# A graph tensor product on one core: other distances between engines in a hand-ordered stage, and one holder for a shared accumulator bank

## The chip, the core and the metric

One core of one Trainium2 chip runs the kernel as one program. Its engines are TensorE (PE: matmuls, whose weight loads have a row PEld of their own), VectorE (DVE), ScalarE (ACT), GpSimd (POOL: here it issues indirect DMAs) and SyncE (SP: it issues plain DMAs). Each engine works off its own list of instructions in order and waits at semaphores for the others. The metric is the device time of one execution in microseconds; lower is better.

## The reference

There are 10000 nodes with 64 channels of 4 components each, and 640000 edges in no order. Every edge takes the row of its source node, forms a small tensor product with its own 4 numbers Y, scales it per channel, and is added to its destination node; at the end the channels are mixed.

```python
N, deg, C, L, DE = 10000, 64, 64, 1, 4          # E = N * deg, M = 4
R = _silu(edge_feat @ w_rad)                              # (E, C)
xs = x[src]                                               # (E, C, M)
tp = jnp.einsum('eci,ef,ifo->eco', xs, Y, cg)             # (E, C, M)
msg = R[:, :, None] * tp
agg = _segment_sum(msg.reshape(-1, C * M), dst, N).reshape(N, C, M)
return jnp.einsum('ncm,cd->ndm', agg, w_mix)
```

## The kernel before

**Sorting.** Edges are brought together by destination in two passes of a radix sort through DRAM. A pass counts, for chunks of 12 tiles of 128 edges, how many edges go to each of 18 digits (`count`, matmuls on one-hots into the bank `cnt`), turns the counts into destinations (`tables`, L290 to L377), and then moves the edges (`route`, L379 to L493). The first pass (`pass1`) sorts by group of 576 nodes and writes to `grp`; the second (`pass2`) sorts a group by bucket of 32 nodes and writes to `bkt`. The edges are handled in two parts, 49% and 51%, so that the first pass over the second part can run beside messages of the first.

**A route** has one chunk per step. `prepare` makes the one-hot D of a quad (two chunks); `places` puts the position of every edge into the accumulator bank `pp` by matmuls, and in the same step ScalarE copies it out as `pc`; `slots` turns it on VectorE into a row and a slot; `spread` builds on VectorE the shifted payload X and most of the one-hots oh, and on ScalarE the last five tiles of oh (squares `sq`, then a ReLU); `move` multiplies them on PE into the bank `pr`; `evict` copies it to `rt` on ScalarE; `store` issues the scatter on POOL, LS = 8 steps after `spread`. In step k the order is evict(k-3), move(k-2), places, spread(k), slots, store(k-8), so X and oh of chunk k take the buffers that move(k-2) gives back where they have two (X), and those of move(k-3) where they have three (oh). `pp` has one buffer and `pr` two, and both are shared by the two routes that run side by side.

**Messages** (`messages`, L644 to L782) go by units: half a bucket, 4 tiles of edges in the first part of the edges and 5 in the second, 626 units in each. Per unit: `gather` issues one indirect DMA per tile on POOL into one of 6 buffers xg; `turn` transposes the payload on PE into a bank `pre` (two buffers), `turned` copies it out on ScalarE as sT, `radial` multiplies it on PE with the radial weights into the same bank, where ScalarE applies SiLU in place; `spots` builds S on VectorE from the destination and Y; `products` multiplies the gathered rows by the radial values in place on VectorE; `sums` adds the unit up on PE in the bank G (one buffer, two units per bucket); `evict` copies G to Gs on ScalarE; every fourth bucket `mix` multiplies by the mixing weights on PE into the bank `po`, and ScalarE or VectorE brings the result to `ot`, which SP writes to the output. A unit is issued in four quarters, in an order written out by hand (L775):

```python
quarters = (((index, LI), (gather, LG), (products, 0), (turn, 1)), ((sums, -1), (turned, 1)),
            ((radial, 1), (spots, 1)), ((evict, -1), (mix, -2)))
```

The number is the unit's offset from the running one.

**What sets the order.** In the main phase (from L931) PE, VectorE and ScalarE take exactly the order in which the program issues; POOL and SP are put in order by a planner. `groups` (L787) issues one quarter of `messages` after another, and ahead of each quarter as many steps of the other two generators as their rates allow: `later` is the first pass over the second part of the edges (about 0.14 steps per quarter, up to the quarter `total`), `sort` is the second pass for the segment that comes next (48 steps over about 144 quarters). In the phase before it only SP keeps the written order. `weave` runs a step of the next block's counting (`front`) beside each step of a first-pass route. All the small matmuls (cnt, offp, ovp, dp, po) share one accumulator bank, "misc"; who comes next waits at its semaphore.

Of the kernel before, what the change touches and what calls it, by code (L numbers as in the profile page):

```python
# [17 lines left out]
F = mybir.dt.float32  # L18
# [6 lines left out]
P = 128  # L25
# [10 lines left out]
LG = 4  # L36
LI = 8
# [15 lines left out]
def weave(main, side, ratio):  # L53

    acc = 0.0
    for _ in main:
# [5 lines left out]
    for _ in side:  # L62
        yield
# [7 lines left out]
class Kernel:  # L71
    def __init__(self, ctx, tc, x, src, dst, Y, ef, w_rad, cg, w_mix, out):
# [49 lines left out]
        self.tab = {}  # L122

# [166 lines left out]
    def tables(self, ps, N, cs, carry, kov, carry2, kov2, base, cap):  # L290
# [14 lines left out]
        yield  # L305
# [47 lines left out]
        yield  # L353
# [14 lines left out]
        yield  # L368
        dp = self.ps.tile([P, 512], F, name="dp", tag="misc", bufs=1)
        nc.tensor.transpose(dp[:, :N], val[:N, :], self.ident[:N, :N])  # L370
        idx = wk.tile([P, P], I32, name="idx", tag="idx" + ps.key, bufs=2)
        ds = dest
        nc.scalar.activation(ds[:, :N], dp[:, :N], AF.Copy)
        yield
# [4 lines left out]
    def route(self, ps, quad, nt, sb, idx):  # L379

        nc, wk, tc, T, Q = self.nc, self.ph, self.tc, ps.T, ps.Q
        N = (nt + T - 1) // T
        QD, PP, MS, XO, PR, RT = {}, {}, {}, {}, {}, {}
# [4 lines left out]
        def places(q):  # L388
# [17 lines left out]
            for u in range(full * T, m - 1):  # L406
# [3 lines left out]
                             Dq.rearrange("p t b -> p (t b)"), start=False, stop=True)  # L410
            pc = PP[q] = wk.tile([P, Q * T, B], F, name="pc", tag="pc" + ps.key, bufs=1)
# [15 lines left out]
        def spread(c):  # L427
# [6 lines left out]
            X = self.ph.tile([P, T, ps.rw], F, name="X", tag="X" + ps.key, bufs=2)  # L434
# [4 lines left out]
            oh = self.ph.tile([P, T, P], F, name="oh", tag="oh" + ps.key, bufs=3)  # L439
# [31 lines left out]
        prepare(0)  # L471
        yield
        places(0)
        yield
        slots(0)
        yield
# [18 lines left out]
    def pass1(self, part, first, size):  # L495
# [16 lines left out]
        def front(o, m):  # L512
# [8 lines left out]
            for a in range(0, m, QT):  # L521
# [3 lines left out]
                yield  # L525
                cnt = self.ps.tile([P, 512], F, name="cnt", tag="misc", bufs=1)
                self.count(cnt, ps, D, a // T, z - a, N, True, True)
                w = min(T, z - a) * B
# [63 lines left out]
    def pass2(self):  # L592
# [11 lines left out]
        for i, (k, g) in enumerate(self.segs):  # L604
# [19 lines left out]
            N = (nt + ps.T - 1) // ps.T  # L624
            cnt = self.ps.tile([P, 512], F, name="cnt", tag="misc", bufs=1)
            for a in range(0, nt, 8 * ps.T):
                z = min(a + 8 * ps.T, nt)
                self.count(cnt, ps, D[:, a:z], a // ps.T, z - a, N, a == 0, z == nt)
            cs = ph.tile([P, ps.T * B], F, name="cs2", bufs=1)
            nc.scalar.activation(cs[:N], cnt[:N, :ps.T * B], AF.Copy)  # L630
            yield
# [8 lines left out]
    def pass2_steps(self, k, g):  # L640
        return (self.gt[k][g] + 27) // 28 + (self.gt[k][g] + 11) // 12 + LS + 20


    def messages(self):  # L644
# [60 lines left out]
        def radial(k):  # L705
# [3 lines left out]
            nc.scalar.activation(R, R, AF.Silu)  # L709
# [45 lines left out]

        def mix(k):
# [211 lines left out]
```

## Time and profile before

| | us |
|---|---|
| median of 3 runs | 10343.14 (10334.53 to 10346.17) |
| the profiled execution | 10335.18, its span 10333.0 |
| PE busy | 8440.1 (82% of the span) |
| VectorE busy | 7318.8 (71%) |
| ScalarE busy | 3553.8 (34%) |
| POOL busy | 6272.0 (61%) |
| gathers: 5634 indirect DMAs | 5345.3, 949 ns each |
| sums: 22536 matmul records | 3202.8 |
| moves of both routes: 21180 matmul records | 2722.7 |

A matmul of this kernel's full precision leaves two records. "Busy" is the time in which an engine has at least one instruction running; PE's ends are modelled. The granted clock (PEclk) is the share of TensorE's full clock that the throttle let through. In the view of waits each row says which engine's instruction waited, for whose, the sum of its waits in us, how many and the longest; a wait for several is put down to the one that came last. A row of the timeline has start, duration, engine, line, operation, the tiles written and read, the count of merged instructions, and in brackets the idle time before it with what ended it.

### The profile page before, as it was taken

The page shows a single profiled execution, that of the slowest core. Times are in us where ns is not written, and L with a number is a line of the kernel's source. Part 1 is how long each engine was busy: PE and PEld are TensorE (multiplying, and loading weights), DVE is VectorE, ACT ScalarE, POOL GpSimd, SP SyncE. Part 2 cuts the span into 40 slices and gives each one's busy share as a digit, 9 for nine tenths or more (in the row PEclk, how much of TensorE's full clock was granted, in tenths as well). Part 3 has the DMA queues.
Part 4 walks back from the last instruction along what each step waited for, and adds up shares of the span by engine and source line. Part 5 has one row for each costly group of instructions (what it writes and reads, how often), then busy time and mean ns, then how long its engine had stood idle before and what let it go on. Part 6 is the DMA issues. An engine that isn't in the chain of part 4 may idle for free. (4 is left out here: it accounts for less than half of the span.)

```text
span 10333.0 us, 160005 instructions
## 1 busy us (share of the span) xinstructions
PE 8440.1 (82%) x58324; PEld 7190.1 (70%) x58324; DVE 7318.8 (71%) x12462; ACT 3553.8 (34%) x11277; POOL 6272.0 (61%) x6576
## 2 busy tenths in 40 slices
PE   6887878878888888788888888888888888888874
PEld 5887667666667667677677777677777777777763
DVE  7998867777677777767776766666666666666643
ACT  3676333333333333333332322222222222222210
POOL 1222546556546556556557777777777777777773
PEclk9999889989989899999999898988899998999986
DMA  3331223223223223223223343333333333333331
GB/s 94 87 89 49 82 70 89 85 78 88 72 64 92 74 81 89 77 71 92 72 78 110 101 116 112 112 113 112 112 112 113 112 112 111 111 111 111 108 115 51
DMA packets 531586, 963.05 MB, mean 93 GB/s; under 512 B 229053, under 2 KB 329720, under 8 KB 530800
## 3 DMA queue, kind: packets, MB, share of 16 engines
q0 software_dynamic: 300464, 790.37, 26.4%
q1 hardware_dynamic: 227744, 149.89, 5.4%
q10 hardware_dynamic: 2592, 12.60, 0.3%
q8 instruction: 458, 7.50, 0.3%
q14 instruction: 328, 2.69, 0.1%
HBM read 830.53 MB, written 131.52 MB: 93 GB/s over the span
## 5 line engine op out<-in xcount | busy, mean ns | idle before, releaser
L685 POOL DMA_INDIRECT xg<-in_x_dram,sidx x5634 | 5345.3, 949 | 2606.3 <-issue 1481.5
L737 PE MATMUL G<-S,xg 128*128 128x128 f32 x22536 | 3202.8, 304 | 258.2 <-ACT Gs L754 253.4
L737 PEld LDWEIGHTS G<-S,xg 128*128 128x128 f32 x22536 | 3066.8, 219 | 335.1 <-ACT Gs L754 310.9
L455 PE MATMUL pr<-X,oh 128*128 128x126 f32 x21180 | 2722.7, 287 | 276.0 <-ACT rt L460 168.2
L455 PEld LDWEIGHTS pr<-X,oh 128*128 128x128 f32 x21180 | 2594.9, 201 | 452.3 <-ACT rt L460 283.0
L726 DVE TENSOR_TENSOR xg<-xg,pre 128x1024 f32<-128x1024 f32 (+1 forms) x1252 | 1689.8, 1350 | 1150.4 <-DMA xg<-in_x_dram,sidx 974.6
L435 DVE TENSOR_TENSOR X<-dv,Wt 128x1512 f32<-128x1512 f32 (+2 forms) x905 | 1532.1, 1693 | 985.6 <-PE pr L455 948.1
L709 ACT ACTIVATE pre<-pre 128x256 f32<-128x256 f32 (+1 forms) x1252 | 494.4, 395 | 3081.6 <-PE pre L708 3019.5
L447 ACT ACTIVATE sq<-i,rowf 128x128 f32<-128x128 f32 x4457 | 1396.4, 393 | 113.1 <-DVE rowf L422 113.0
L719 DVE TENSOR_TENSOR S<-dv,pay 128x512 f32<-128x512 f32 (+1 forms) x1252 | 949.5, 758 | 443.4 <-PE G L737 351.6
L708 PE MATMUL pre<-wr,sT 36*128 36x256 f32 (+1 forms) x2504 | 994.9, 479 | 174.1 <-ACT sT L703 172.0
L463 POOL DMA_INDIRECT grp<-rt,idx x417 | 412.4, 989 | 892.1 <-ACT rt L460 583.0
L442 DVE TENSOR_TENSOR oh<-dv,rowf 128x896 f32<-128x896 f32 x887 | 948.4, 1069 | 0.0
L698 PE MATMUL pre<-ident,pay 128*36 128x128 f32 (+1 forms) x1252 | 384.5, 307 | 642.8 <-DVE xg L726 638.6
L698 PEld LDWEIGHTS pre<-ident,pay 128*36 128x36 f32 (+1 forms) x1252 | 139.4, 111 | 982.9 <-DVE xg L726 817.9
L412 ACT ACTIVATE pc<-pp 128x432 f32<-128x432 f32 (+3 forms) x454 | 234.6, 517 | 1498.7 <-PE pp L409 1457.7
L463 POOL DMA_INDIRECT bkt<-rt,idx x488 | 488.1, 1000 | 429.9 <-ACT rt L460 258.5
L448 ACT ACTIVATE oh<-sq,ones 128x640 f32<-128x640 f32 (+1 forms) x905 | 739.8, 817 | 23.4
L765 PE MATMUL po<-wf,Gs 128*128 128x256 f32 (+2 forms) x2784 | 667.1, 394 | 11.7 <-DVE cs L529 10.9
L703 ACT ACTIVATE sT<-pre 36x128 f32<-36x128 f32 (+1 forms) x1252 | 328.4, 262 | 910.2 <-PE pre L698 905.3
L708 PEld LDWEIGHTS pre<-wr,sT 36*128 36x128 f32 (+1 forms) x2504 | 394.6, 197 | 348.2 <-ACT sT L703 208.5
L765 PEld LDWEIGHTS po<-wf,Gs 128*128 128x128 f32 (+2 forms) x2784 | 499.9, 185 | 177.0 <-issue 65.2
(176 smaller groups left out, 5233.8 us busy)
## 6 DMA issues: line engine op xcount, KB each, us to landing
xg<-in_x_dram,sidx POOLq DMA_INDIRECT x5634
bkt<-z SPq DMA_DIRECT2D x26, 972.0 KB
out_dram<-ot SPq DMA_DIRECT2D x138, 128.0 KB
pay<-bkt SPq DMA_DIRECT2D x17, 810.0 KB
grp<-z SPq DMA_DIRECT2D x17, 738.0 KB
Wt<-grp SPq DMA_DIRECT2D x17, 738.0 KB
grp<-z ACTq DMA_DIRECT2D x17, 706.5 KB
Wt<-grp SPq DMA_DIRECT2D x17, 706.5 KB
```

What stands on the lines that cost most here:

```text
L435: nc.vector.tensor_tensor(X[:, :m, :].rearrange("p t (s w) -> p t s w", w=W), msk.unsqueeze(3).to_broadcast([P, m, ps.r, W]), QD[c // Q][1 ...
L442: nc.vector.tensor_tensor(oh[:, :v, :], self.v128.unsqueeze(1).to_broadcast([P, v, P]), row[:, a:a + v].unsqueeze(2).to_broadcast([P, v, P ...
L447: nc.scalar.activation(sq[:, u - v, :], self.i128, AF.Square, bias=row[:, a + u:a + u + 1], scale=-1.0)
L448: nc.scalar.activation(oh[:, v:m, :], sq[:, :m - v, :], AF.Relu, bias=self.ones[:, 0:1], scale=-2.0)
L455: nc.tensor.matmul(pr[:, :ps.rw], oh[:, u, :], X[:, u, :], start=(u == 0), stop=(u == m - 1))
L463: st = nc.gpsimd.indirect_dma_start(out=ps.dst, out_offset=bass.IndirectOffsetOnAxis(ap=idx[:, c:c + 1], axis=0), in_=RT.pop(c), in_offset ...
L685: nc.gpsimd.indirect_dma_start(out=xg[:, t, :], out_offset=None, in_=self.x, in_offset=bass.IndirectOffsetOnAxis(ap=si[:, u:u + 1], axis=0))
L708: nc.tensor.matmul(R, ST_.pop(k)[:ut * W], self.wr[:ut * W, :ut * 64], start=True, stop=True)
L719: nc.vector.tensor_tensor(S[:, :ut], self.eq[:, :ut].unsqueeze(3).to_broadcast([P, ut, NB, 4]), pb[:, :, 1:5].unsqueeze(2).to_broadcast([P ...
L726: nc.vector.tensor_tensor(V, V, R.unsqueeze(3).to_broadcast([P, ut, 64, 4]), op=OP.mult)
L737: nc.tensor.matmul(G[:, h].rearrange("p n f -> p (n f)"), V[:, t, 32 * h:32 * h + 32, :].rearrange("p c i -> p (c i)"), S[:, t].rearrange( ...
L765: nc.tensor.matmul(po[:nn, :256], Gs[:, h, f].rearrange("p b n -> p (b n)")[:, :nn], self.wf[:, h, f, :], start=(h + f == 0), stop=(h + f ...
```

## The change

In `messages` the quarters and the units' offsets are dealt out anew; `radial` and its SiLU, `mix` and its copy become two stages each. In `route` the copy of the placement bank becomes a stage of its own (`placed`), one step after `places`; `prepare` comes one step before `places`; the route begins four steps ahead of its first chunk. `pp` gets a holder (`self.pos`): while one route has it, the other yields "held". The shared bank "misc" gets one too (`self.held`, and `self.wanted` for the mix); `bank()` yields only while another has it. Where a yield stood ahead of a matmul into that bank, `bank()` stands now, and a yield comes after the matmul. In the main phase X has two buffers in the first pass's route and three in the second's, oh two and three (before: two and three in both); in the phase before, three and three. The steps' rates follow.

```diff
+    def bank(self):
+        while self.held or self.wanted:
+            yield "held"
+        self.held = True
...
         nc.vector.tensor_copy(R[:N], ri[:N])
-        yield
+        yield from self.bank()
         off_p = self.ps.tile([P, 512], F, name="offp", tag="misc", bufs=1)
...
+        yield
         off, ot = w("off", B), w("ot", B)
         nc.scalar.activation(off[:N], off_p[:N, 0:B], AF.Copy)
         nc.scalar.activation(ot[0:1], off_p[0:1, 64:64 + B], AF.Copy)
+        self.held = False
...
+        def placed(q):
+            m = min(Q * T, nt - q * Q * T)
+            pp = PS.pop(q)
             pc = PP[q] = wk.tile([P, Q * T, B], F, name="pc", tag="pc" + ps.key, bufs=1)
             nc.scalar.activation(pc[:, :m, :], pp[:, :m, :], AF.Copy, bias=-BIG)
...
-            X = self.ph.tile([P, T, ps.rw], F, name="X", tag="X" + ps.key, bufs=2)
+            X = self.ph.tile([P, T, ps.rw], F, name="X", tag="X" + ps.key, bufs=self.xb[ps.key])
...
-            oh = self.ph.tile([P, T, P], F, name="oh", tag="oh" + ps.key, bufs=3)
+            oh = self.ph.tile([P, T, P], F, name="oh", tag="oh" + ps.key, bufs=self.xb[ps.key])
...
-        prepare(0)
-        yield
-        places(0)
-        yield
-        slots(0)
-        yield
-        NQ = (N + Q - 1) // Q
-        for k in range(N + LS):
-            if k % Q == 0 and k // Q + 1 < NQ:
-                prepare(k // Q + 1)
+        for k in range(-2 * Q, N + LS):
             if 0 <= k - 3 < N:
                 evict(k - 3)
             if 0 <= k - 2 < N:
                 move(k - 2)
-            if k % Q == max(Q // 2 - 1, 0) and k // Q + 1 < NQ:
-                places(k // Q + 1)
-            if k < N:
+            if k % 2 and 0 <= k + 3 < N:
+                while self.pos:
+                    yield "held"
+                self.pos = True
+                places((k + 3) // 2)
+            if k % 2 == 0 and 0 <= k + 2 < N:
+                placed((k + 2) // 2)
+                self.pos = False
+            if k % 2 == 0 and 0 <= k + 4 < N:
+                prepare((k + 4) // 2)
+            if 0 <= k < N:
                 spread(k)
-            if k % Q == Q - 1 and k // Q + 1 < NQ:
-                slots(k // Q + 1)
+            if (k + 1) % 2 == 0 and 0 <= k + 1 < N:
+                slots((k + 1) // 2)
...
                 self.onehot(D[:, :z - a], da[:, a:z], z - a)
-                yield
+                yield from self.bank()
                 cnt = self.ps.tile([P, 512], F, name="cnt", tag="misc", bufs=1)
                 self.count(cnt, ps, D, a // T, z - a, N, True, True)
+                yield
+                self.held = False
...
-        quarters = (((index, LI), (gather, LG), (products, 0), (turn, 1)), ((sums, -1), (turned, 1)),
-                    ((radial, 1), (spots, 1)), ((evict, -1), (mix, -2)))
-        for k in range(-LI, n + 2):
+        quarters = (((index, LI), (gather, LG), (turn, 2), (sums, 0), (silu, 1)), ((turned, 2), (spots, 1)),
+                    ((products, 1), (evict, 0)), ((radial, 2), (full, -1)))
+        todo, po = [], None
+        for k in range(-LI, n + 3):
             for stages in quarters:
                 for f, a in stages:
                     if 0 <= k + a < n:
                         f(k + a)
                 yield
+                if po is not None:
+                    mixed(todo.pop(0), po)
+                    po, self.held = None, False
+                elif todo and not self.held:
+                    self.held, self.wanted = True, False
+                    po = mix(todo[0])
...
-        rate = (nch + 5 * (LS + 4) + 50) / total
+        rate = (nch + 6 * (LS + 4) + 60) / total
...
+            acc1 += rate
+            while acc1 >= 1.0 or v >= total:
+                acc1 -= 1.0
+                if next(later, "end") in ("end", "held"):
+                    break
...
-                    next(sort)
+                    if next(sort) == "held":
+                        break
...
+            self.xb = {"grp": 3}
...
+            self.xb = {"grp": 2, "bkt": 3}
```

The two other banks of `tables` (ovp, dp) and the second pass's cnt are treated like offp; `pass2_steps` goes from LS + 20 to LS + 24; `full(k)` puts a finished quad of buckets on the list `todo` and sets `self.wanted`.

More of the change, by code (lines that the diff above doesn't have):

```diff
@@ L60, in weave @@
             next(side, None)
-        yield
-    for _ in side:
-        yield
+        yield said
+    yield from side
 def run(gen):
@@ L367, in tables @@
         nc.vector.tensor_tensor(val[:N], val[:N], rk[:N], op=OP.add)
-        yield
+        yield from self.bank()
         dp = self.ps.tile([P, 512], F, name="dp", tag="misc", bufs=1)
         nc.tensor.transpose(dp[:, :N], val[:N, :], self.ident[:N, :N])
+        yield
         idx = wk.tile([P, P], I32, name="idx", tag="idx" + ps.key, bufs=2)
@@ L524, in front @@
                 self.onehot(D[:, :z - a], da[:, a:z], z - a)
-                yield
+                yield from self.bank()
                 cnt = self.ps.tile([P, 512], F, name="cnt", tag="misc", bufs=1)
                 self.count(cnt, ps, D, a // T, z - a, N, True, True)
+                yield
+                self.held = False
                 w = min(T, z - a) * B
@@ L624, in pass2 @@
             N = (nt + ps.T - 1) // ps.T
+            yield from self.bank()
             cnt = self.ps.tile([P, 512], F, name="cnt", tag="misc", bufs=1)
@@ L766, in mix, with mixed @@
                                      self.wf[:, h, f, :], start=(h + f == 0), stop=(h + f == 4))
+            return po
+        def mixed(k, po):
+            g, j, s = units[k]
+            n0, nn = quad(k)
             ot = ph.tile([P, 256], F, name="ot")
@@ L815, in groups @@
                     acc -= 1.0
-                    next(sort)
-                if v >= ends[i]:
+                    if next(sort) == "held":
+                        break
+                if v >= ends[i] and segs[i + 1] in self.pay:
                     i, start, acc = i + 1, ends[i], 0.0
```

32 lines of the change are left out of this document (17 added, 15 removed).

## The prediction

> **What bounds the kernel now.** I read the busy time by stage first, then who waited for whom in the second and third stages, then one stretch of the timeline. Stages: the first pass over half of the edges (0 to 1000 us), messages of the first half beside the first pass over the other half (to 5400, "stage A"), messages with bucket sorting alone ("stage B", to 10180), the overflow loop.
>
> ```profile
> core 0: us, PE busy (x) PEld busy (x) DVE busy (x) ACT busy (x) POOL busy (x), PEclk, DMA share, GB/s
> 0.00:1000.00 1000.00, 798.50 (x6618) 728.52 (x6618) 922.93 (x1941) 603.25 (x1761) 201.92 (x218) 0.95 0.29 81
> 1000.00:5400.00 4400.00, 3581.96 (x25036) 3044.31 (x25037) 3221.96 (x5616) 1626.60 (x5218) 2443.78 (x2549) 0.91 0.28 79
> 5400.00:10180.00 4780.00, 4015.42 (x26542) 3388.99 (x26540) 3124.85 (x4698) 1316.90 (x4270) 3603.49 (x3787) 0.90 0.38 111
> 10180.00:10333.00 153.00, 44.23 (x131) 28.30 (x131) 49.04 (x209) 7.08 (x30) 22.83 (x23) 0.53 0.04 11
> ```
>
> ```profile
> DVE xg L726 <- DMA xg<-in_x_dram,sidx: 926.3, 315, 7.2
> POOL xg L685 <- issue: 912.4, 2995, 0.3
> ...
> PE pre L698 <- DVE xg L726: 467.8, 247, 5.8
> ```
>
> The second fence is from the waits between 5600 and 10150 us. In stage B POOL issues 3787 indirect DMAs in 4780 us, one per 1.26 us: 0.95 busy and 0.3 until the next one issues, and it waits for nothing else of any size. The products wait for gathers (926.3 us), and PE for the products (467.8). Stage B runs at POOL's pace, and the change adds no DMA and takes none away. The first stage is VectorE's, 922.93 of 1000 us, and there a planner orders all engines but SP. So the question is stage A. Its waits between 1100 and 5350 us, first the longest of all engines, then VectorE's, then all of PE's over 10 us:
>
> ```profile
> ACT pre L709 <- PE pre L708: 1033.0, 482, 9.1
> ACT pc L412 <- PE pp L409: 950.2, 202, 15.1
> POOL xg L685 <- PE G L737: 842.3, 254, 12.3
> ```
>
> ```profile
> DVE X L435 <- PE pr L455: 741.0, 239, 8.5
> DVE S L719 <- PE G L737: 202.1, 148, 7.4
> ```
>
> ```profile
> PE pr L455 <- ACT rt L460: 164.2, 143, 3.8
> PE pre L698 <- DVE xg L726: 157.5, 60, 9.4
> PE G L737 <- ACT Gs L754: 125.5, 115, 3.2
> PE pre L708 <- ACT sT L703: 114.0, 99, 4.2
> PE pp L404 <- DVE D L278: 77.8, 30, 9.1
> PE cnt L285 <- DVE Da L278: 39.1, 11, 10.5
> PE ovp L355 <- DVE rk L352: 34.6, 11, 5.7
> PE dp L370 <- DVE val L367: 21.8, 6, 5.2
> PE offp L307 <- DVE R L304: 11.9, 6, 4.2
> ```
>
> POOL waits 842.3 us there for a gather buffer that the sums on PE give back: PE with its helpers sets the pace. PE is busy 3582 of 4400 us (81%), VectorE 73%, POOL 56%. PE's idle time has two owners: ScalarE (164.2 + 125.5 + 114.0 = 404 us) and VectorE (157.5 + 77.8 + 39.1 + 34.6 + 21.8 + 11.9 = 343 us). ScalarE and VectorE wait for PE far longer, but that costs only what comes back as a wait of PE. So I price the change in waits of PE in stage A.
>
> **The change, part by part.** No instruction and no DMA is added or removed. Each moves in an order that PE, VectorE and ScalarE follow strictly. "Distance" below is how many quarters of a unit lie in that order between producer and consumer; a unit in stage A takes 4250 / 520 = 8.2 us, a quarter 2 us (520 units: the products' row in the next fence).
>
> *ScalarE behind PE: better.* Evicting the placement bank (pc) leaves the step of its matmuls and comes one route step later, before the squares of the one-hots; SiLU comes one quarter after its matmul, the mix's copy too; turned to radial goes from one quarter to two. Now a pc that waits for PE is followed by 5 squares and a ReLU before ScalarE comes to the rt that PE needs. That is what feeds the 404 us. One new wait goes the other way: with two buffers instead of three for the group route's one-hots, ScalarE's ReLU waits for the move of its own step. Bounds: 0 to -404. The eviction to the sums keeps its two quarters and rt still comes in the step of its move, so I keep 110 of the 404: **-290**.
>
> *Prepare one step before places: better.* Today the onehot D of a quad and the matmuls on it share a step. Bounds 0 to -77.8; the distance becomes a whole step, so **-78**.
>
> *Products and spots closer to the sums: worse.* Products to sums goes from five quarters to two, products to the turn that takes their bank from four to two, spots to sums from seven to three. VectorE lags wherever a route's X waits for the move of the same step (741.0 us), as it still will in the group route (two X buffers); in the bucket route a third X buffer ends that, and S gains distance (202.1).
>
> ```profile
> L726 DVE TENSOR_TENSOR xg<-xg,pre 128x1024 f32<-128x1024 f32 x520 | 631.3, 1214 | 75.1 <-ACT pre L709 52.0 <-DMA xg<-in_x_dram,sidx 17.7 <-issue 1.8
> ...
> L334 DVE TENSOR_SCALAR steps<-dv,st,dd 14x128 f32<-14x128 f32 (+3 forms) x357 | 118.5, 391 | 0.0
> ...
> L278 DVE TENSOR_TENSOR Da<-dv,da 128x432 bf16<-128x432 f32 (+1 forms) x108 | 62.9, 583 | 0.0
> ```
>
> These are groups of stage A's instructions by line. From the single rows behind the first I took, unit by unit, the end of its products against the start of the next unit's radial matmul, which stands two quarters later today: in 165 of 519 units PE is there first, by 432 us in all. At today's four quarters that lag costs 157.5. So the new distance costs between -157 (VectorE no longer late) and 432 - 157 = +275; with half of the X waits and all S waits gone, I take the middle of zero and the upper end: **+140**.
>
> *Counts and tables: worse.* A free bank yields no step. So where a yield stood between VectorE's result and PE's matmul (onehot to cnt in the front; R to offp, rk to ovp, val to dp in the tables), nothing stands now, and the step goes behind the matmul. The timeline at one front step, VectorE and then PE:
>
> ```profile
> 1859.01 1.73 DVE L435 TENSOR_TENSOR X<-dv,Wt 128x1512 f32<-128x1512 f32 x1 [2.15 <-PE pr L455]
> 1860.66 1.08 DVE L442 TENSOR_TENSOR oh<-dv,rowf 128x896 f32<-128x896 f32 x1
> ...
> 1863.10 0.59 DVE L278 TENSOR_TENSOR Da<-dv,da 128x432 bf16<-128x432 f32 x1
> ```
>
> ```profile
> 1858.90 0.36 PE L285 MATMUL cnt<-Da,sel 128*39 128x216 bf16 x2
> ...
> 1864.88 0.40 PE L698 MATMUL pre<-ident,pay 128*36 128x128 f32 x1 [2.83 <-DVE xg L726]
> ```
>
> PE counts at 1858.90 what VectorE made a step earlier; VectorE, whose X had to wait for PE's move, ends this step's Da at 1863.69, 4.4 us after PE could have used it. In the new order PE stands there until then, with the next turn, sums and everything else queued behind. Over the 101 front steps of stage A whose route runs beside them (108 Da in all) this lag sums to 303 us, 3.0 each, 43 of them longer than 3.77 us. Upper bound +303; lower 0, where VectorE was about to hold PE up anyway, as in the last row (2.83 us). But all such waits together come to 157.5 now, so most of it is new: **+200**. The tables: 357 / 17 = 21 of them, three such points each, at 34.6 / 11 = 3.1 us (what PE waits at rk where it does wait, with a step between): upper bound 195, lower 0 (the bank is held by another, or VectorE is ahead). In the middle: **+100**. In stage B the 18 or so tables hold PE up too, but that is covered by POOL's gather lead; without the cover it would be 18 x 3 x 3.1 = 167 us.
>
> *At nothing.* The shared bank's holder and the placement bank's holder only postpone steps: the group route holds the latter for one of its steps, some 6.7 quarters, and the bucket route loses a step or two each time; it has 52 steps where it needs about 46, and the payload's load lies several units ahead of its use. The added step per route is covered by the higher rates. The mix's output DMA goes out on SP one quarter later, and nobody waits for it before the buffer comes round. Gathers and stores keep their places; buffers free three quarters earlier, which POOL cannot use while PE sets the pace. First stage: a third X buffer, priced -10 to +10 under VectorE's 92%.
>
> *Sum.* -290 - 78 + 140 + 200 + 100 = +72 us on the profiled run's 10335.2 us (span 10333.0 plus 2.2), whose time lies 8 below the median of 10343.1: **10415 us**.
>
> [...] Two moves of one chunk, from the timeline at 3000 us:
>
> ```profile
> 3007.29 4.57 PE L455 MATMUL pr<-X,oh 128*128 128x126 f32 x24 [3.77 <-ACT rt L460]
> ...
> 3016.80 2.94 PE L455 MATMUL pr<-X,oh 128*128 128x126 f32 x24 [1.15 <-ACT rt L460]
> ```
>
> After 3.77 us of idleness the same 24 matmuls take 1.63 us longer than after 1.15. If each of the 43 lags at the counts that are longer than that 3.77 does so, 43 x 1.63 = 70 us come on top. [...]
>
> **Rivals.**
>
> 1. *Faster.* VectorE, rid of the bucket route's X waits and of S, runs ahead of PE, so products, counts and tables are ready when PE comes. Then the 404, 77.8 and 157.5 go but for 110, and counts and tables cost half, 150: -379, **9965 us**. For it: VectorE is only 73% busy. Against: the group route's X still waits for PE in the very step whose Da PE then needs, so VectorE cannot be ahead there. It decides if PE's waits on VectorE stay under 290 us in stage A.
> 2. *Slower by the clock.* The sum plus 70: **10485**. For it: the two rows above. Against: long waits behind ScalarE go away at the same time.
> 3. *No change.* The waits only change owners: **10343**. For it: the distances round the loop turn, radial, products, turn add up to eight quarters in both orders, two banks' worth.
> 4. *Stage B loses POOL's pace.* PE has no slack left behind products that land late, and sums give the buffers back too late. If PE's 467.8 us for late products come a second time and two thirds of that get past POOL, that is +312: **10727**. Against: POOL had no wait for a buffer there, and it decides only once POOL has.
>
> **How the numbers follow.** Forecast 10415 with its own range 10350 to 10470: 0.47. Rival 1: 0.31; rival 2: 0.09; rival 3: 0.07; rival 4: 0.06. All gains without a loss would be -639, all losses without a gain +773 (303 + 275 + 195). The range runs from 9930, past rival 1, to 10700, past rival 2 and short of rival 4; what is left outside is under a fifth, mostly rival 1's lower end. About 0.2% (20 us) is what a measurement of this kernel can tell from no change. Faster by more: 0.31 plus 0.01 from the forecast's edge = 0.32; within: 0.07; slower: 0.61.
>
> **What would show it.** Right: in stage A ScalarE's waits for PE at pc and SiLU fall by more than half, PE's waits for rt, Gs and sT to about 110 us, D at the placement matmuls vanishes; cnt waiting for Da rises from 39 to some 250, offp, ovp and dp from 68 to about 170 together, and turn or sums waiting for products to about 300; X waits for PE remain at the group route only; stage B keeps its 3787 DMAs at 1.26 us. Wrong: counts that wait under 80 us in all (rival 1), a lower granted clock in stage A than 0.91 (rival 2), or POOL waiting for PE in stage B (rival 4).

## The result and the profile after

The changed kernel takes 10414.87 us (median of 4 runs, 10413.06 to 10420.19), the kernel before 10344.65 us on the same chip: 1.0070 times as long, 95% interval 1.0053 to 1.0088. The profiled execution has a span of 10412.3 us, 79.3 more than before. By stage, in the same columns as before:

```profile
core 0: us, PE busy (x) PEld busy (x) DVE busy (x) ACT busy (x) POOL busy (x), PEclk, DMA share, GB/s
0.00:1000.00 1000.00, 803.72 (x6668) 719.56 (x6669) 922.88 (x1950) 600.39 (x1778) 202.01 (x218) 0.96 0.29 81
1000.00:5400.00 4400.00, 3591.84 (x24427) 3067.67 (x24426) 3147.50 (x5508) 1583.43 (x5068) 2411.92 (x2513) 0.87 0.27 79
5400.00:10260.00 4860.00, 4065.22 (x27103) 3457.35 (x27102) 3193.90 (x4798) 1396.79 (x4403) 3648.18 (x3822) 0.89 0.38 110
```

In the 4400 us of stage A VectorE finishes 5508 instructions instead of 5616, and the granted clock is 0.87 instead of 0.91. The loss lies there: the products of the first unit end at 1102.5 us (before 1111.0), those of unit 625 at 6043.7 (before 5974.0), and the units behind take 4217 us (before 4208). So -8 us in the first stage, +78 in units 0 to 625, +9 behind them. From here on stage A is looked at as "units 0 to 625", which holds the same work in every kernel, from the end of the first unit's products to the end of unit 625's. The windows view of just this stretch, first before, then after:

```profile
1111.00:5974.00 4863.00, 4002.41 (x27824) 3395.17 (x27824) 3534.32 (x6123) 1752.63 (x5678) 2820.23 (x2945) 0.91 0.29 83
```

```profile
1102.50:6043.70 4941.20, 4082.85 (x27831) 3489.46 (x27831) 3530.94 (x6123) 1765.90 (x5678) 2824.35 (x2945) 0.88 0.28 82
```

PE's idle time is the length less the busy time: 4863.0 - 4002.4 = 860.6 us before, 4941.2 - 4082.9 = 858.3 after. **PE waits just as long as before; what grew by 80 us is its busy time, for the same 27.8 thousand records.** The same windows for the sums alone (PE, PEld and ScalarE on the bank G), before and after:

```profile
1111.00:5974.00 4863.00, 1387.78 (x9993) 1317.15 (x9994) 136.80 (x624) 0.91 0.29 83
```

```profile
1102.50:6043.70 4941.20, 1505.59 (x10000) 1451.16 (x10000) 137.26 (x624) 0.88 0.28 82
```

The same ten thousand sums take 118 us longer, and PE's other work 37 us less. Who waits for whom in stage A after the change (1100 to 5350 us, as before), first the longest of all engines, then PE's. (This window is fixed, so it holds somewhat less of a slower kernel's work. Summed over units 0 to 625 instead, the products' wait goes from 185.0 to 372.7 us and the counts' from 38.2 to 195.5; the reading is the same.)

```profile
DVE X L453 <- PE pr L473: 792.4, 191, 10.6
POOL xg L709 <- PE G L763: 748.2, 226, 12.7
ACT pre L735 <- PE pre L732: 735.8, 365, 14.7
ACT oh L466 <- PE pr L473: 572.3, 176, 15.3
```

```profile
PE pre L722 <- DVE xg L752: 308.4, 116, 10.1
PE cnt L291 <- DVE Da L284: 195.5, 62, 11.2
PE po L795 <- DVE cs L550: 63.5, 23, 3.1
PE ovp L363 <- DVE rk L360: 49.1, 9, 11.7
PE pr L473 <- ACT rt L478: 45.5, 62, 3.6
PE offp L313 <- DVE R L310: 35.9, 9, 8.0
PE dp L380 <- DVE val L377: 32.0, 8, 6.4
PE pre L732 <- ACT sT L727: 13.0, 12, 1.9
```

ScalarE's share of PE's waits is nearly gone (404 us before, some 60 now); VectorE's has taken its place, at the products, the counts and the mix. The new waits have another shape: rt cost 164.2 us in 143 waits of 1.15 us, the counts cost 195.5 us in 62 waits of 3.2 us. One such step on the timeline, VectorE and then PE:

```profile
1976.95 1.73 DVE L453 TENSOR_TENSOR X<-dv,Wt 128x1512 f32<-128x1512 f32 x1 [8.18 <-PE pr L473]
1978.60 1.08 DVE L460 TENSOR_TENSOR oh<-dv,rowf 128x896 f32<-128x896 f32 x1
1979.60 0.36 DVE L550 TENSOR_TENSOR cs<-cs,cnt 39x216 f32<-39x216 f32 x1
1979.88 0.59 DVE L284 TENSOR_TENSOR Da<-dv,da 128x432 bf16<-128x432 f32 x1
```

```profile
1974.07 2.84 PE L473 MATMUL pr<-X,oh 128*128 128x126 f32 x24
1980.53 0.34 PE L291 MATMUL cnt<-Da,sel 128*39 128x216 bf16 x2 [3.62 <-DVE Da L284]
1980.80 1.22 PE L732 MATMUL pre<-wr,sT 36*128 36x256 f32 x2
1982.72 0.40 PE L722 MATMUL pre<-ident,pay 128*36 128x128 f32 x1 [0.70 <-DVE xg L752]
1982.91 3.66 PE L763 MATMUL G<-S,xg 128*128 128x128 f32 x16
```

PE ends the move at 1976.91, which frees the buffer for VectorE's X; X, oh, cs and Da follow one another, and only then can PE count. So this chain sets the length of the wait, 3.62 us, and it comes again and again: 22 of the 62 waits at the counts last between 3.5 and 3.7 us. The sums behind it take 3.66 us, and the clock records have half clock there from 1980.83 to 1991.07 us. Of the sixteen-matmul sums of units 0 to 625 in this kernel, the 84 that lie wholly at half clock take 3.62 us in the median, the 434 wholly at full clock 1.95.

Stage B, from 5700 to 10240 us:

```profile
DVE xg L752 <- DMA xg<-in_x_dram,sidx: 1064.9, 328, 6.7
...
POOL xg L709 <- issue: 923.0, 3027, 0.3
...
PE pre L722 <- DVE xg L752: 683.1, 341, 6.3
```

PE waits more for the products there (467.8 us before), but POOL still waits for hardly anything but its own issue: for the sums 20.9 us after and 25.4 before. The pace of stage B is POOL's in both kernels.

### The profile page after: what moved, and what is told of

It reads as the page before. It is cut to its first block, busy times and chain, and to the rows that moved or that the text cites. A ratio compares the mean times of both kernels' runs of the same rounds, so it can differ in the third digit from the quotient of the medians.

```text
span 10412.3 us, 159949 instructions
## 1 busy us (share of the span) xinstructions
PE 8505.1 (82%) x58324; PEld 7273.0 (70%) x58324; DVE 7312.6 (70%) x12462; ACT 3587.7 (34%) x11277; POOL 6285.0 (60%) x6576
## 5 line engine op out<-in xcount | busy, mean ns | idle before, releaser
L763 PE MATMUL G<-S,xg 128*128 128x128 f32 x22536 | 3329.7, 313 | 5.8 <-DVE dv L742 2.7
L763 PEld LDWEIGHTS G<-S,xg 128*128 128x128 f32 x22536 | 3218.0, 228 | 24.1 <-issue 4.2
L473 PE MATMUL pr<-X,oh 128*128 128x126 f32 x21180 | 2644.8, 282 | 148.1 <-DVE oh L460 85.9
L473 PEld LDWEIGHTS pr<-X,oh 128*128 128x128 f32 x21180 | 2525.4, 197 | 278.6 <-DVE oh L460 97.5
L732 PE MATMUL pre<-wr,sT 36*128 36x256 f32 (+1 forms) x2504 | 1024.4, 492 | 13.6 <-ACT sT L727 13.6
L795 PE MATMUL po<-wf,Gs 128*128 128x256 f32 (+2 forms) x2784 | 681.0, 400 | 65.9 <-DVE cs L550 63.5
L780 ACT ACTIVATE Gs<-G 128x128 f32<-128x128 f32 x1252 | 276.0, 272 | 1068.8 <-PE G L763 1068.7
L417 PE MATMUL pp<-D,onesb 128*128 128x396 bf16 (+14 forms) x4983 | 540.7, 257 | 12.6 <-DVE D L284 12.6
```

What stands on the lines that cost most here:

```text
L473: nc.tensor.matmul(pr[:, :ps.rw], oh[:, u, :], X[:, u, :], start=(u == 0), stop=(u == m - 1))
L732: nc.tensor.matmul(R, ST_.pop(k)[:ut * W], self.wr[:ut * W, :ut * 64], start=True, stop=True)
L763: nc.tensor.matmul(G[:, h].rearrange("p n f -> p (n f)"), V[:, t, 32 * h:32 * h + 32, :].rearrange("p c i -> p (c i)"), S[:, t].rearrange( ...
L795: nc.tensor.matmul(po[:nn, :256], Gs[:, h, f].rearrange("p b n -> p (b n)")[:, :nn], self.wf[:, h, f, :], start=(h + f == 0), stop=(h + f ...
```

## The experiments

Each kernel was timed beside the kernel before on the same chip; ratios are to that kernel, and differences are given in points of them (one point is a hundredth, 103 us); the kernel before had medians of 10325 to 10345 us beside them. The numbers of PE in units 0 to 625 come from the windows view of each run. "Waits over 2 us" counts PE's idle gaps there of 2 us or more. Waits of one row are again taken from 1100 to 5350 us, which holds more of a faster kernel's work; over units 0 to 625 PE waits for the products 185 us before, 373 after, and 517 in e1, 588 in e3, 249 in e4, 629 in e6, 409 in e7 and 241 in e8.

| run | median us | ratio (95%) | length | PE idle | PE busy | clock | waits over 2 us |
|---|---|---|---|---|---|---|---|
| before | 10344.65 | 1 | 4863 | 861 | 4002 | 0.914 | 139 |
| after | 10414.87 | 1.0070 (1.0053-1.0088) | 4941 | 858 | 4083 | 0.876 | 191 |
| e1_front | 10173.40 | 0.9843 (0.9827-0.9860) | 4712 | 758 | 3954 | 0.898 | 154 |
| e2_tables | 10322.23 | 0.9988 (0.9979-0.9998) | 4856 | 832 | 4024 | 0.888 | 183 |
| e3_both | 10163.96 | 0.9836 (0.9820-0.9853) | 4699 | 749 | 3950 | 0.899 | 152 |
| e4_quarter | 10331.39 | 0.9999 (0.9989-1.0009) | 4863 | 819 | 4044 | 0.886 | 177 |
| e5_route | 9891.33 | 0.9581 (0.9565-0.9597) | 4428 | 587 | 3841 | 0.942 | 73 |
| e6_quarters | 10666.30 | 1.0329 (1.0312-1.0346) | 5191 | 1051 | 4140 | 0.868 | 216 |
| e7_shift | 10026.48 | 0.9707 (0.9691-0.9723) | 4561 | 646 | 3915 | 0.912 | 125 |
| e8_lag | 9595.91 | 0.9292 (0.9277-0.9308) | 4133 | 386 | 3747 | 0.950 | 62 |
| e9_route_lag | 9675.74 | 0.9372 (0.9358-0.9387) | 4210 | 440 | 3770 | 0.959 | 50 |
| e10_silu | 9646.45 | 0.9345 (0.9331-0.9359) | 4178 | 399 | 3779 | 0.955 | 47 |
| e11_fill | 10346.38 | 1.0024 (1.0015-1.0033) | 4878 | 793 | 4085 | 0.893 | 176 |
| e12_oldbufs | 9906.14 | 0.9595 (0.9580-0.9610) | 4439 | 597 | 3843 | 0.940 | 77 |

In every run the units behind 625 take 4207 to 4218 us: stage B moves by 11 us at most, and all that follows is stage A.

**e1_front: the yield in `front` back ahead of the count.**

```diff
                 self.onehot(D[:, :z - a], da[:, a:z], z - a)
+                yield
                 yield from self.bank()
...
-                yield
                 self.held = False
```

> The changed kernel with one part undone: in the front the step stands ahead of the count again, and the bank is given back in the count's own step. Background for all four runs: over the first 625 units PE's idle time is the same in the two kernels (862 and 859 us), and its busy time for the same matmuls rose from 4001 to 4082 us. Theory C (long waits cost twice): single waits of PE have become longer (81 of 3.4 us or more against 44), the granted clock falls and the matmuls take longer. Then this run loses most of the 62 waits of cnt for Da (195 us, 3.2 us each): about half of it moves to products, PE idle of units 0 to 625 about 780, busy about 4040, time about 10295. Theory M (waits only change owners, the clock has another cause): cnt's 195 us come back as waits for products (308 to about 500), idle and busy as in the changed kernel, time 10400 to 10430.

PE's waits in stage A, this kernel:

```profile
PE pre L722 <- DVE xg L752: 479.3, 172, 11.7
...
PE cnt L291 <- DVE Da L284: 31.6, 9, 9.5
```

The time falls by 2.3 points, more than either theory gave. The counts give up 164 us of waiting, and the products take 171 us more in this window (145 over units 0 to 625), as theory M had it: VectorE is late all the same, and PE now meets it at the next place. But PE's idle and busy time both fall, as theory C had it. What fell is the number of waits over 2 us (191 to 154), PE's busy time (4083 to 3954) and PE's idle time in the whole stretch (858 to 758).

**e2_tables, e3_both: the yields in `tables` back ahead of the three matmuls, alone and together with e1's.**

```diff
+        yield
         yield from self.bank()
...
-        yield
```

> The changed kernel with one part undone: in the tables the step stands ahead of the matmuls into the shared bank again (offp, ovp, dp), and ScalarE copies them out in their own step. Theory C: PE's waits there (36 + 49 + 32 = 117 us in stage A) fall to some 60; time about 10415 - 60 - 20 = 10335. Theory M: 10400 to 10430. If the copies, again in the step of their matmuls, make ScalarE late, PE's waits for rt, Gs and sT rise above their 60 us.

> The changed kernel with both parts undone (front and tables), so that only the new quarters, the new order inside a route, the buffers and the bank's holder are left. Theory C: the two gains add up, PE idle of units 0 to 625 about 720, busy about 4020, time about 10220, faster than the kernel before. Theory M: 10400 to 10430.

The tables alone are worth 0.8 points (1.0070 to 0.9988); behind the counts they are worth nothing that can be told (0.9843 and 0.9836, with intervals that overlap). The two gains do not add up, as theory C expected them to. A likely reason is that both are places at which the same lag of VectorE is met; no run shows that by itself.

**e4_quarter, e7_shift: one quarter more from products to sums.** In e4 on the changed kernel, in e7 on e3_both.

```diff
-        quarters = (((index, LI), (gather, LG), (turn, 2), (sums, 0), (silu, 1)), ((turned, 2), (spots, 1)),
-                    ((products, 1), (evict, 0)), ((radial, 2), (full, -1)))
+        quarters = (((index, LI), (gather, LG), (silu, 1)), ((turn, 2), (sums, 0), (spots, 1)),
+                    ((products, 1), (turned, 2)), ((radial, 2), (evict, 0), (full, -1)))
```

> The changed kernel with turn, sums, turned and evict one quarter later in a unit, so that products stand three quarters ahead of the turn and the sums instead of two, and ScalarE's copy of the turned payload one quarter ahead of the radial matmul instead of two. Front and tables stay as in the change. Theory C: PE's waits for products (308 us in stage A, 2.7 us each) fall to about 200, waits for sT rise from 13 to some 60, time about 10415 - 60 - 30 = 10325. Theory M: 10400 to 10430.

> The change without its front and tables parts (10164 us), and with turn, sums, turned and evict one quarter later, so that products stand three quarters ahead of them. There PE waits 550 us for products in stage A, nearly all of its idle time. If the distance is what is short, these waits fall by a third or more, as they did in the changed kernel (308 to 208), and the time to 10060 to 10100. If VectorE's work as such is the limit there (it lags because its X waits for the group route's move), the waits stay above 480 us and the time above 10130.

One quarter is worth 0.7 points on the changed kernel (its products' waits fall from 308.4 to 207.9 us, those at rk rise from 49.1 to 98.2) and 1.3 points on e3_both (550.4 to 384.4 us, somewhat less than the third that was expected, while the time came out below the 10060 to 10100 us).

**e5_route: the change in `route` alone** (`placed`, `prepare` one step earlier, the holder of `pp`, the buffers of X and oh, the rates), with the quarters, the front and the tables of before.

> The kernel before with one part of the change: the new order inside a route (placed a step after places, prepare a step ahead of places, the placement bank's holder, X and one-hot buffers, the rates). Quarters, mix, tables and front stay as before. Question: whence come the 166 us by which the change without its front and tables parts beats the kernel before. Theory R (the route): ScalarE no longer stands at pc, so PE's waits for rt, Gs and sT fall from 404 us to below 200, D at the placement matmuls from 78 to about 0; time 10150 to 10230. Theory Q (the quarters): those waits stay above 300, because SiLU still waits in the step of its matmul; time 10290 to 10340.

PE's and VectorE's waits in stage A of this kernel, two views:

```profile
PE pre L705 <- DVE xg L733: 215.6, 101, 9.4
PE pr L461 <- ACT rt L466: 115.1, 143, 4.1
PE G L744 <- ACT Gs L761: 69.2, 108, 2.5
...
PE pre L715 <- ACT sT L710: 26.6, 21, 3.2
```

```profile
DVE X L441 <- PE pr L461: 316.8, 141, 5.8
```

This part alone makes the kernel 4.2 points faster. Its waits are about those of theory R, its time far below the 10150 to 10230 us given there. It halves what PE waits for ScalarE (404 to 211 us), D is gone from the list, and X waits for PE 316.8 us instead of 741.0.

**e6_quarters: the rest without it**: e3_both with the route of before, so the new quarters, the splits of SiLU and mix and the shared bank's holder (the rates stay as changed).

> The change without its front and tables parts, and with the route of the kernel before (two X and three one-hot buffers in both routes, pc in the step of its matmuls): only the new quarters, the split mix and the shared bank's holder are left. Theory R: PE's waits for rt stay near 164 us and D at the placement matmuls near 78, and products at two quarters cost as much as SiLU's new distance brings; time 10290 to 10380. Theory Q: 10150 to 10230.

The same two views of this kernel:

```profile
PE pre L715 <- DVE xg L745: 537.9, 177, 10.5
```

```profile
DVE X L447 <- PE pr L467: 1093.2, 246, 11.1
```

It is the slowest of all, 3.3 points over the kernel before, and neither theory had it (10380 us was the highest). VectorE's X waits longer for PE than in any other (741.0 us before), and PE for the products more than three times as long as before (157.5). Put together: route alone -4.2; quarters, mix and holder on top of it +2.6 (0.9581 to 0.9836); front and tables on top of that +2.3 (0.9836 to 1.0070); in all +0.7. **The small result is the sum of large parts of both signs.**

**e8_lag: e7_shift with the group route's move one step behind its spread instead of two**, its store one step earlier, the same buffers. X and oh of chunk k then take the buffer of a move that PE was given one step before, and no longer that of the move which stands right ahead of it.

```diff
-            if 0 <= k - 3 < N:
-                evict(k - 3)
-            if 0 <= k - 2 < N:
-                move(k - 2)
+            if 0 <= k - d - 1 < N:
+                evict(k - d - 1)
+            if 0 <= k - d < N:
+                move(k - d)
...
+            self.lag = {"grp": 1, "bkt": 2}
```

> The run with the shifted quarter, and in the main phase the group route's move one step behind its spread instead of two (its store one step earlier too): with the same two buffers X and the one-hots then wait for a move of the step before, not of their own. If VectorE lags behind PE because of that wait (700 us at X, 540 us of ScalarE at the one-hots), both fall by more than half, PE's waits for products to below 250 us, and the time to 9960 to 10040. If not, PE waits instead at the move, one step behind its X, and the time stays within 30 us of the run with the shifted quarter alone.

The waits for the move in stage A, first of e7, then of this kernel:

```profile
DVE X L453 <- PE pr L473: 612.5, 189, 9.6
ACT oh L466 <- PE pr L473: 593.4, 185, 15.4
```

```profile
DVE X L453 <- PE pr L473: 11.0, 11, 2.2
```

X waits 11.0 us instead of 612.5 in e7 (792.4 in the changed kernel), ScalarE's wait for the same move at oh is gone as well, and the kernel becomes 4.2 points faster than e7. The edit ends both waits at once, and no run parts them. This is the fastest kernel of the study, 0.9292 of the time before (0.9277 to 0.9308), and well under what was expected.

**e9_route_lag, e10_silu: the same edit on e5_route; and on that SiLU one quarter behind its matmul.**

> The route part of the change alone, on the old quarters, with the group route's move one step behind its spread instead of two, and its store one step earlier. Theory N (distances that differ by engine: the fewer things a buffer's giver stands behind, the less VectorE's lag comes back to PE; the same edit took 430 us off the kernel with the new quarters): the X waits of 317 us vanish and PE's waits for the products fall below 130 us in stage A; 9550 to 9750 us. Theory O (the move of one step now stands right behind its own spread, which the old quarters with five quarters from products to sums do not need): PE waits for X or oh for over 150 us; 9850 to 10050 us.

> The kernel of the run beside it (route part alone, old quarters, move one step behind spread) with SiLU one quarter later than its matmul. Theory N (ScalarE's 1326 us of waiting for the radial matmul delay what PE needs next from ScalarE): PE's waits for rt, Gs and sT, some 210 us before the edit, halve; 60 to 120 us less than the run beside it. Theory P (ScalarE's waiting costs nothing, and a later SiLU delays the products that the sums wait for): the products' wait rises by 30 to 100 us and the time by 0 to 80 us.

PE's waits in stage A of e9:

```profile
PE pre L705 <- DVE xg L733: 133.2, 66, 8.2
PE pr L461 <- ACT rt L466: 93.3, 129, 2.5
PE G L744 <- ACT Gs L761: 74.4, 124, 2.0
```

The edit is worth 2.1 points here, X waits 5.9 us, and theory N's numbers hold to within 3 us of the products' wait. SiLU's quarter brings 0.3 points, in the direction of theory N but at less than half of its price and with intervals that just touch: rt, Gs and sT together fall from 186 to 149 us, and the products wait 10 us longer. Seen beside e7 and e8: with X and oh waiting for the move the new quarters, shifted, lose 1.3 points to the old ones (0.9707 against 0.9581); without those waits they win 0.8 (0.9292 against 0.9372). So short distances from products to sums seem not to be dear in themselves, but where VectorE is late. The two sides also differ in SiLU, mix and the bank's holder, so this is not shown for the distances alone.

**e11_fill: the clock by itself.** In the changed kernel, in those steps of the group route in which the front counts, 14 more matmuls that add zeros to the bank of the move.

```diff
+            more = 14 if self.fill and ps.key == "grp" and "bkt" in self.xb else 0
...
+            for u in range(more):
+                nc.tensor.matmul(pr[:, :ps.rw], self.sel[:, :P], self.onesb[:, :ps.rw], start=False,
+                                 stop=(u == more - 1))
```

> The changed kernel with 14 more matmuls that add zeros at the end of the group route's move, in those steps in which the front counts, some 1.5 us of PE work in place of idleness ahead of about 110 counts. Theory C (the idle lags at the counts lower the granted clock and so lengthen the work behind them): cnt's waits fall by 80 to 130 us, the granted clock in stage A rises by 0.005 or more, the busy time of all other matmuls falls, and the time falls by 10 to 60 us. Theory M (the loss is the order: what is late stays late): cnt's waits fall by as much as PE's own work rises, or by less, the time rises by 20 to 80 us, and the other matmuls' busy time stays within 10 us.

PE at one such step, and the windows row of units 0 to 625:

```profile
1942.80 0.93 PE L477 MATMUL pr<-onesb,sel 128*128 128x126 bf16 x14
...
1947.85 0.34 PE L291 MATMUL cnt<-Da,sel 128*39 128x216 bf16 x2 [2.52 <-DVE Da L284]
...
1948.88 1.95 PE L770 MATMUL G<-S,xg 128*128 128x128 f32 x16
```

```profile
1101.20:5979.00 4877.80, 4084.97 (x29161) 3506.81 (x29161) 3527.53 (x6123) 1763.96 (x5678) 2816.24 (x2944) 0.89 0.29 83
```

PE does 1330 more matmuls, and the kernel becomes faster, from 1.0070 to 1.0024, with intervals that do not overlap. The moves' bank is busy 78 us longer, PE as a whole 2 us: the other matmuls take 76 us less. The granted clock rises from 0.876 to 0.893. The counts wait 161.0 us instead of 195.5, in 62 waits as before: the 22 of 3.62 us last 2.85 now, and the row shows one of the shorter kind. Its sums take 1.95 us, the median at full clock in the changed kernel, but they are among the best: over all 62 counts the sixteen sums behind take 3.03 us on average, instead of 3.28. Theory C holds in time (0.46 points, 47 us), clock and busy time; the fill, 0.93 us, was shorter than the 1.5 us it was put at, and the counts' waits fell by 35 us, not by 80 to 130. Undoing the front (e1) gains more than this, so the clock is one part of the counts' price, and the waiting itself the other.

**e12_oldbufs: e5_route with the buffers of before.**

```diff
-            X = self.ph.tile([P, T, ps.rw], F, name="X", tag="X" + ps.key, bufs=self.xb[ps.key])
+            X = self.ph.tile([P, T, ps.rw], F, name="X", tag="X" + ps.key, bufs=2)
...
-            oh = self.ph.tile([P, T, P], F, name="oh", tag="oh" + ps.key, bufs=self.xb[ps.key])
+            oh = self.ph.tile([P, T, P], F, name="oh", tag="oh" + ps.key, bufs=3)
```

> The route part alone, with the buffers of the kernel before in the main phase and the phase ahead of it: X two, oh three in both routes. Theory B (the gain of 439 us of the route part comes from the third X buffer of the bucket route): the X waits return to some 700 us, and the time to 10150 to 10300 us. Theory P (it comes from pc leaving the step of its matmuls and from D one step earlier): 9850 to 9980 us, with SiLU's and pc's waits as in the route part alone.

VectorE's wait at X in stage A of this kernel:

```profile
DVE X L441 <- PE pr L461: 420.7, 222, 5.9
```

0.9595 and 0.9581 cannot be told apart, so the gain is not the buffers'. It comes from the rest of the route's part: pc and D, whose waits are gone, with the placement bank's holder and the rates, which no run parts from them. X waits 420.7 us here, against 316.8 with the new buffers and 741.0 before, so most of X's waiting went without the third buffer. The new buffers also bring ScalarE a wait at oh, 284.5 us in e5 and none here; that may be why X's gain is not seen in the time.

## Why the prediction came out

The time was forecast at 10415 us and is 10414.87, inside the forecast's own range. That it came so near is luck, as the sum of the terms shows, each in PE's waits of stage A (1100 to 5350 us):

| term | forecast | measured | how |
|---|---|---|---|
| ScalarE behind PE | -290 | -344 | 404 to 45.5 + 13.0 + 1.0 (rt, sT, Gs) |
| prepare ahead of places | -78 | -78 | gone from the list |
| products and spots closer | +140 | +151 | 157.5 to 308.4 |
| counts in the front | +200 | +156 | 39.1 to 195.5 |
| tables | +100 | +49 | 68.3 to 117.0 |
| mix behind cs, not priced | 0 | +53 | 10.9 to 63.5 |
| sum | +72 | -13 | |

Over units 0 to 625, the same work in both kernels, the measured rows are -380, -78, +188, +157, +53 and +53, and all of PE's idle time changes by -2 us.

**The signs and the owners were right.** Every view that was to change did: pc fell from 950.2 to 37.9 us and SiLU from 1033.0 to 735.8, three fifths of the two together, though SiLU alone fell by three tenths only. X waited at the group route, which the change gives no third buffer: e8 shows whose waits they are, as there they go with an edit of that route alone. But the forecast let half of the X waits and all S waits go, and X rose from 741.0 to 792.4 while S kept 111.0 of 202.1. So the +140 for the products came from a premise that failed. Stage B kept its pace, 3822 indirect DMAs in 4860 us, one per 1.27.

**The sum was right by two misses that cancel.** The waits come to 85 us less than forecast, by the rows of the table; rival 3, waits that only change owners, describes them best. The time is there because the same matmuls take 80 us longer, which is what rival 2 had, with its sign: the granted clock of stage A is 0.87, under 0.91. The step that failed is the one that prices the change in waits of PE alone, with every matmul at its old length.

The clock records show what the clock has in this. Of PE's busy time in units 0 to 625, 722 us lie in stretches at half clock before and 1012 after. With half of that taken off (an estimate, that work takes twice as long there; the sums take 3.62 us at half clock and 1.95 at full), 3641 us are left before and 3577 after. The seven other runs with the new quarters and no fill leave 3573 to 3587 us, the four others with the old quarters 3630 to 3638. So here PE's busy time is an amount that goes with the order of the quarters, plus half of what falls into half clock. By that estimate the clock adds 145 us, and the new order needs 64 less at full clock; no run shows why it does.

The rows to do better stood in the prediction: a move of 4.57 us behind a wait of 3.77, and of 2.94 behind one of 1.15, a difference of 1.63. The clock records of the kernel before have half clock from 3007.66 to 3011.08 us, so in 3.41 us of the first move, and none in the second (PEclk 0.63 and 1.00 in the windows of the two rows). The prediction put the difference on 43 lags and gave that a small chance. It belongs into the sum, as a change in the number of long waits: in units 0 to 625 those over 2 us went from 139 to 191. For the 52 more of them the clock's share, 145 us, is 2.8 each; that 52 x 1.63 = 85 us lies near the 80 measured is luck again. e11 shows that this is a cause and not a companion: more work of PE, put where it shortens the waits, and less time. There PE's busy time at half clock falls from 1012 to 858 us, and half of that difference, 77 us, is what the other matmuls gain (76).

**The sizes of the parts were off.** Undone one by one they are larger than their own rows of waits.

- Route: -368 forecast for all that goes better, of which e5 has only the route's share; alone it is worth 4.2 points, 433 us. Half of ScalarE's waits (193 us) and D's 78 explain 271 of it; PE's busy time falls by another 161.
- Quarters: +140 forecast beside a share of the -290; measured +2.6 points on the new route and +3.3 on the old. The bound of +275 for the products failed: in e3 and e6 they wait 550.4 and 537.9 us, 380 to 393 more than before. It was made with VectorE's lag as it was before; but X waits for PE, and PE for the products, so a distance made shorter makes VectorE later too (X in e6: 1093.2 us). That this loop is the reason fits e8, where X no longer waits and the products wait 247.6; it was not measured by itself. In the changed kernel the products' +151 came out near the forecast only because counts and tables stop PE ahead of them; with those undone it is +393.
- Counts and tables: +300 forecast, 2.3 points or 242 us measured together. Undoing the counts alone brings 235 of them.

**Rival 1** failed where the prediction said it would be decided: PE waits for VectorE 684 us in stage A (308.4 + 195.5 + 63.5 + 49.1 + 35.9 + 32.0), far over 290; in the step on the timeline the group route's X waits for PE just ahead of the Da that PE needs. e8 and e9 show the other half of that argument: with the waits for that move away, and front and tables as before, the kernel is faster than rival 1 said. **Rival 4** did not come: PE lost its slack behind the gathers (467.8 to 683.1 us of waiting for the products), but POOL waited no more for PE than before (20.9 and 25.4 us). The first stage moved by 8 us, within its bounds.

## What to carry to other kernels

In an order that several engines follow strictly, a wait moves to the next place at which the same late engine is met, so find out first why it is late: here buffers given back in the step that wants them cost 4.2 points with the new quarters (e8) and 2.1 with the old (e9), as much as whole parts of the change. Price a wait of TensorE by its length as well as by its sum: here waits of about 1 us (rt: 143 of 1.15) gave way to fewer of about 3 (the counts: 62 of 3.2), PE's idle time stayed (861 and 858 us), and the same matmuls took 80 us longer. And when a change of many parts moves the time by less than a percent, undo it part by part before judging any of them; here its best part alone is 4.2% faster than the kernel it was made from.

## What the runs showed of the hardware

The granted clock takes only two values in the records of the kernel before (676 stretches) and of the changed one (734), 1.0 and 0.5, and the stretches are, but for the last of each run, whole multiples of 3.413 us; in units 0 to 625 the half clock holds for 2 x (1 - 0.914) x 4863 = 836 us before and 2 x (1 - 0.876) x 4941 = 1225 us after. Half clock came behind waits shorter than one such stretch too. Taking only waits of PE in the changed kernel that began at full clock, some half clock within the next 4 us came behind 7 of 97 waits of 0.1 to 1 us, 22 of 57 of 1 to 2 us, 41 of 54 of 2 to 3 us, 47 of 50 of 3 to 3.4 us, and all 83 longer ones. (In the first two classes it can be due to a later wait.) That is why the waits were counted from 2 us on: over the kernels with the new quarters PE's busy time follows that number, from 3747 us at 62 such waits to 4140 at 216, some 2.6 us for each. The others with the new quarters keep within 32 us of the line between these two (e11 without the 78 us of its fill), and the five with the old ones lie 54 to 71 us above it, about the difference at full clock found above.
